# A memory-augmented transformer step on one core: an own buffer for the last head outputs of every fourth segment, and two steps of left-row work at other spots

## The chip, the cores and the metric

The kernel runs on one core of one Trainium2 chip. The metric is device time in microseconds (us), lower is better. Each time is one execution of the whole program; "before" is the median of three such runs. A profile is one further execution, with the hardware profiler on; it has its own, slightly longer time. Engines are named as in the profile: PE (TensorE, matmuls; PEld its weight loads), ACT (ScalarE), DVE (VectorE), POOL (GpSimd), SP (SyncE, which issues nearly all DMAs here; SPq in the profile).

## The reference, cut to what matters

```python
# x: 2048 tokens x 640; 32 heads of 192; segments of 32 tokens, 8 memory rows
for s in range(64):
    h = concatenate([mem, x[:, 32*s:32*s+32]])         # 40 rows
    q, k, v = h @ Wq, h @ Wk, h @ Wv                   # 40 x 32 heads x 192
    p = softmax(where(mask, q @ k.T / sqrt(192), -1e9))
    o = (p @ v) @ Wo                                   # 40 x 640
    mem = o[:, :8]                                     # the next segment needs this
    outs.append(o[:, 8:])
a = concatenate(outs)
b = (gelu(x @ w_gate) * (x @ w_up)) @ w_down
out = sigmoid((x * gate_w).sum(-1)) * a + (1 - that) * b
```

Segments form a chain: the first projection of a segment waits for the eight memory rows of the one before. The feed-forward part `b` is done ahead of the chain and isn't touched.

## The kernel before, in words

**Rows.** Of the 40 rows of a segment, the chain does 32 at once (24 tokens and the 8 memory rows). The last 8 tokens of a segment, its *left rows*, don't depend on the memory for their own queries, keys and values; they are done for four segments together, 32 rows again. Four segments make a group of places 0, 1, 2 and 3 (`q = s % 4`); there are 16 groups.

**Octets.** The 32 heads go through in four octets of eight heads, forwards in even segments, backwards in odd ones.

**Order.** Each segment walks a list written out by hand: `PROG` for places 0 and 2, `PROG1` (the same but for one item) for place 1, `PROG3` for place 3. Engines run their instructions in the order in which the list issues them; a layer records reads and writes of each region of on-chip memory and puts in the semaphore waits. Where a PE step waits for several engines, that layer may move all but one of the waits onto the last matmuls of the step in front. The items are

- `g n k`: step k (of 5) of projection group n, for queries, keys and values of some octets: four matmuls each (L1134, and L226 where the weights in the array are kept). When step 4 is done, ACT copies the result out (L1155 queries and keys, L1158 values)
- `tq`, `tk`: 32 x 32 transposes of queries and keys on DVE (L1172)
- `sc`, `ex`, `pt`: scores (PE, L1183 to L1198), softmax (DVE, ACT), transposes of the probabilities (PE, L1245 and L1250; ACT L1257 and L1263)
- `pv o`: probabilities times values of octet o (PE, L1278 and L1280, 12 matmuls on tiles of 128 x 64), and the copies of the head outputs to on-chip memory (ACT L1310 or, in two halves, L1300; DVE L1315 or, in two halves, L1304)
- `wo o h`: half of the output projection of octet o. At places 0 to 2 it takes 32 rows (PE, L1328; L1354 for the fourth octet, tiles of 128 x 32). At place 3 it is `wo_both` (PE, L1372, tiles of 128 x 64, 12 matmuls a half): 32 rows and the 32 left rows of the group, 64 columns of weights
- `lf x u k`: at place x alone, one of five steps of the queries and keys of left rows of the next group (a *left pair*: four matmuls at L926 and four at L226, tiles of 128 x 32); `le` copies the result out (ACT L1400, DVE L1402)
- `vb k`: at place 3, one of five steps of the left rows' values for the next segment (PE, L967, four matmuls on tiles of 128 x 32), copied out by ACT at L958

**Head outputs.** At places 0 to 2 two buffers `uT` alternate between octets, and the fourth octet is copied in two halves (two pairs of heads each), by ACT and DVE in parallel, so that the output projection can begin after the first. At place 3 there is one buffer, `U3` (1536 bytes a partition, 64 columns per head pair and part), over both `uT` buffers; POOL copies the left rows' head outputs of the group from `uTl` into its columns 40 to 64 (L1292), and ACT and DVE copy the octet in one piece each. As every octet uses the same buffer, the PV copies of octet o wait for the output projection of octet o - 1, and the list has `wo o-1 1` ahead of `pv o`.

**End of a segment.** After the last output projection the result is copied out (at place 3 ACT L1564 and DVE L1561), transposed on DVE (L1572) and becomes the memory rows of the next segment's first projection (L1134 again).

**Weights.** They don't all fit. In each segment 13 pieces of Wq, Wk and Wv and 3 of Wo are loaded over pieces that were used early in it, by SP (L631); each load waits for the last use of the slot and is used near the end of the segment. The three of Wo follow `wo 0 0` (two) and `wo 0 1` (one).

Of the kernel before, what the change touches and what calls it, by code (L numbers as in the profile page):

```python
# [238 lines left out]
def _build(nc, A_x, A_mem0, A_Wq, A_Wk, A_Wv, A_Wo, seg_len, w_gate, w_up, w_down,  # L239
# [124 lines left out]
    def sreg(o, nbytes, plo=0, phi=128):  # L364
        return Rg("sb", o, o + nbytes, plo, phi)
# [63 lines left out]
    r_U3p = [[sreg(wsB_off["uT"] + x + 4 * i, 4) for x in (0, UB)] for i in range(3)]  # L429
    st_f = [[fview(wsA_off["stats"] + (2 * b + i) * 16, 16) for i in (0, 0, 1)] for b in range(2)]  # L430
# [87 lines left out]
    def piece_view(key, o):  # L518
        if key[0] == 3:
# [76 lines left out]
    o = 0  # L596
# [669 lines left out]
    def pv_oct(s, o):  # L1266
# [23 lines left out]
        if q == 3:  # L1290
            u, ru = U3, r_U3p
            S_.add("pool", lambda e: e.tensor_copy(  # L1292
                out=U3.rearrange("p t c r -> p (t c) r")[:, :, R:64], in_=uTl[:, 12 * oc:12 * oc + 12, :]),
                reads=[r_uTl[oc]], writes=r_U3p[2], name="U3l s%d o%d" % (s, o))
        if o == NOCT - 2 and s + 1 < NSEG:
            ek_copy(s, (3,))
        if o == NOCT - 1 and q < 3:
            assert na == 2 and o % NUB == 1 and WOP == 4
            for h in ((0, 1), (1, 0))[s % 2]:
                S_.add("act", lambda e, h=h: e.activation(  # L1300
                    out=apx(u[:, 2 * h, 0, :], [[R, 2], [3 * R, 2], [1, R]]),
                    in_=ps[:, A, 0:2 * W].rearrange("p (c t r) -> p c t r", t=4, r=R)[:, :, 2 * h:2 * h + 2], func=ACTF.Copy),
                    reads=[r_ps[A]], writes=[r_uThp[h][0]], name="uT evac s%d o%d" % (s, o))
                S_.add("dve", lambda e, h=h: e.tensor_copy(  # L1304
                    out=u[:, 2 * h:2 * h + 2, 2, 0:R],
                    in_=ps[:, B, 2 * W:3 * W].rearrange("p (t r) -> p t r", r=R)[:, 2 * h:2 * h + 2]),
                    reads=[r_ps[B]], writes=[r_uThp[h][1]], name="uT mid s%d o%d" % (s, o))
# [60 lines left out]
    def wo_both(s, item):  # L1368
        for p in wo_pairs(s, item):
            g_, rg_ = piece(s, (3, p))  # L1370
            for c in range(3):
                S_.add("pe", [lambda e, i=i, g_=g_, c=c, p=p: e.matmul(  # L1372
                    ps[64 * i:64 * i + 64, LB, 0:2 * DJ], U3[:, p % 4, c, :], g_[:, c, 2 * DJ * i:2 * DJ * (i + 1)],
                    start=(p == NWP - 1 and c == 0), stop=(p == 0 and c == 2), tile_position=(0, 64 * i),
                    skip_group_check=True) for i in range(2)],
                    reads=[rg_, r_U3], writes=[r_ps[LB]], name="Wb s%d p%d" % (s, p))
# [4 lines left out]
    for x, prog in enumerate(PROGS):  # L1381
# [4 lines left out]
        assert all(at(("wo", i, 1)) < at(("pv", i + (1 if x == 3 else 2))) for i in range(NOCT - (1 if x == 3 else 2)))  # L1386
# [279 lines left out]
```

## Time and profile before

| what | before |
|---|---|
| three timed runs, median (lowest to highest) | 1659.49 us (1658.9 to 1665.99) |
| profiled execution: its time | 1669.24 us |
| profiled execution: span from first to last instruction | 1667.5 us |
| mean granted PE clock | 0.996 |
| the 64 segments in the span | from about 257.5 us to the end |
| the output matmuls of place 3 (L1372) | 1536, mean 307 ns, 122.6 us busy |
| POOL's copy of left rows at place 3 (L1292) | 64 of 128 x 288, 429 ns |
| loads of weight pieces, issue to landing (median) | 5.5 us Wq, 6.5 us Wk, 8.7 us Wv, 6.0 us Wo |

How to read it: the page gives busy time, share of the span and count per engine; the chain of waits follows the work that ended last back from the end. Timelines have rows of start (us from the start of the span), length (us), engine, line of the kernel, operation, tiles and count, and, in brackets, how long the engine had been idle before and what released it. Matmuls of one kind that follow each other are one row; matmuls are pipelined, so starts are better to calculate with than ends. Segment 25 (place 1), 26 (place 2) and 27 (place 3) start at 758.34, 780.83 and 803.58 us, segment 28 at 826.74.

### The profile page before, as it was taken

How to read it: one execution, taken by the hardware profiler on the slowest of the kernel's cores; microseconds unless marked ns; L12 is line 12 of the kernel's file. 1: busy time of each engine (PE TensorE's matmuls, PEld its weight loads, DVE VectorE, ACT ScalarE, POOL GpSimd, SP SyncE). 2: the span in 40 equal slices, each digit the busy share in tenths (PEclk: the TensorE clock that was granted, in tenths of full speed). 3: DMA queues.
4: the chain of work that ended last, by engine and by line, in shares of the span. 5: the costliest groups of instructions: out<-in, count | busy, mean ns of one | idle time of the engine just before them, and what ended most of it. 6: DMA issues, size and time to landing. Idle time of an engine off the chain costs nothing.

```text
span 1667.5 us, 75813 instructions
## 1 busy us (share of the span) xinstructions
PE 1566.5 (94%) x37107; PEld 779.2 (47%) x28147; DVE 1000.1 (60%) x3023; ACT 785.5 (47%) x1874; POOL 549.9 (33%) x1609
## 2 busy tenths in 40 slices
PE   9999899999999999999999999999999999999986
PEld 4444345444444445444455444454444454444533
DVE  6453566656566666666565666566665656656653
ACT  2222454545555454545455554455454555545442
POOL 1110233333333333333333333333333333333332
PEclk9999999999999999999999999999999999999999
DMA  9915899888889898988889898889888898888984
GB/s 297 340 43 160 323 321 330 301 282 310 324 317 325 300 319 290 334 306 311 303 305 343 315 327 289 303 315 340 308 302 310 308 336 311 307 297 308 324 312 179
DMA packets 275415, 499.28 MB, mean 299 GB/s; under 512 B 121119, under 2 KB 136327, under 8 KB 275079
## 3 DMA queue, kind: packets, MB, share of 16 engines
q1 hardware_dynamic: 271000, 491.30, 84.2%
q8 instruction: 255, 4.18, 1.0%
q10 hardware_dynamic: 4079, 3.14, 0.6%
q14 instruction: 81, 0.66, 0.1%
HBM read 473.25 MB, written 21.09 MB: 296 GB/s over the span
## 4 chain that ended last, share of the span: by engine, by line
PE 71%; DMA 17%; DVE 6%; ACT 3%; issue 3%; SPq 1%; POOL 0%; DVEq 0%; ACTq 0%; POOLq 0%
PE ps L1134 19%; PE ps L226 17%; DMA arena<-in_A_Wv_dram 9%; PE ps L1372 7%; DMA arena<-in_A_Wo_dram 6%; PE ps L1328 5%; PE ps L1278 3%; PE ps L835 3%; PE ps L832 3%; PE ps L1354 2%; PE ps L1183 2%; PE ps L926 2%; PE ps L858 2%; PE ps L1191 1%; DMA arena<-in_A_Wk_dram 1%
## 5 line engine op out<-in xcount | busy, mean ns | idle before, releaser
L1134 PE MATMUL ps<-arena 128*32 128x384 bf16 x8640 | 645.6, 328 | 28.0 <-DVE arena L1572 11.6
L226 PE MATMUL ps<-arena 128*32 128x384 bf16 x8960 | 639.7, 326 | 2.7 <-ACT arena L1155 1.2
L1134 PEld LDWEIGHTS ps<-arena 128*32 128x32 bf16 x8640 | 231.9, 96 | 399.2 <-issue 258.9
L1172 DVE STREAM_TRANSPOSE arena<-arena 128x384 bf16<-128x384 bf16 x512 | 273.6, 559 | 70.5 <-ACT arena L1155 69.3
L1155 ACT ACTIVATE arena<-ps 128x384 bf16<-128x384 f32 x512 | 230.4, 493 | 99.0 <-PE ps L1134 93.8
L1328 PE MATMUL ps<-arena 128*32 128x320 bf16 x3456 | 184.4, 300 | 16.2 <-issue 11.1
L1175 POOL COPY arena<-arena 64x160 bf16<-64x160 bf16 x256 | 81.9, 320 | 334.3 <-DVE arena L1172 332.8
L1210 DVE TENSOR_REDUCE arena<-ps 104x4 f32<-104x160 f32 x256 | 82.9, 324 | 162.3 <-PE ps L1198 162.0
L1158 ACT ACTIVATE arena<-ps 128x384 bf16<-128x384 f32 x256 | 124.9, 488 | 88.2 <-PE ps L1134 88.2
L1263 ACT ACTIVATE arena<-ps 128x448 bf16<-128x448 f32 x192 | 104.4, 544 | 125.3 <-PE ps L1250 125.3
L1222 ACT ACTIVATE ps<-ps 104x160 f32<-104x160 f32 x256 | 74.8, 292 | 177.0 <-DVE ps L1212 175.2
L1310 ACT ACTIVATE arena<-ps 128x480 bf16<-128x480 f32 (+1 forms) x208 | 116.7, 561 | 87.4 <-PE ps L1280 86.1
L1008 POOL COPY arena<-arena 128x96 bf16<-128x96 bf16 x256 | 70.2, 274 | 246.7 <-PE ps L1198 174.4
L1224 DVE TENSOR_REDUCE arena<-ps 104x4 f32<-104x160 f32 x256 | 82.9, 324 | 83.8 <-ACT ps L1222 82.4
L1372 PE MATMUL ps<-arena 128*64 128x320 bf16 x1536 | 122.6, 307 | 0.5 <-ACT arena L1310 0.5
L1278 PE MATMUL ps<-arena 128*64 128x160 bf16 x1536 | 116.9, 240 | 5.6 <-ACT arena L1155 3.4
L1328 PEld LDWEIGHTS ps<-arena 128*32 128x32 bf16 x3456 | 89.6, 96 | 62.2 <-issue 19.1
L926 PE MATMUL ps<-arena 128*32 128x384 bf16 x1280 | 109.6, 328 | 1.1 <-issue 0.8
L1280 PE MATMUL ps<-arena 128*64 128x64 bf16 x1536 | 103.7, 193 | 2.3 <-issue 1.9
L1400 ACT ACTIVATE arena<-ps 128x384 bf16<-128x384 f32 x120 | 57.3, 490 | 101.2 <-PE ps L926 48.9
L1318 POOL COPY arena<-arena 128x96 bf16<-128x96 bf16 x192 | 51.7, 270 | 159.8 <-ACT arena L1300 88.7
L1278 PEld LDWEIGHTS ps<-arena 128*64 128x64 bf16 x1536 | 81.2, 109 | 37.6 <-ACT arena L1158 14.4
(102 smaller groups left out, 2362.6 us busy)
## 6 DMA issues: line engine op xcount, KB each, us to landing
arena<-in_A_Wk_dram SPq DMA_DIRECT2D x335, 384.0 KB, 6.5
arena<-in_A_Wv_dram SPq DMA_DIRECT2D x335, 384.0 KB, 8.7
arena<-in_A_Wo_dram SPq DMA_DIRECT2D x205, 480.0 KB, 6.0
arena<-in_A_Wq_dram SPq DMA_DIRECT2D x209, 384.0 KB, 5.5
arena<-left_qk_scratch SPq DMA_DIRECT2D x126, 96.0 KB
left_qk_scratch<-arena SPq DMA_DIRECT2D x49, 192.0 KB, 5.4
left_qk_scratch<-arena SPq DMA_DIRECT2D x30, 96.0 KB, 5.5
ffn_b_scratch<-arena ACTq DMA_DIRECT2D x16, 160.0 KB, 4.1
```

The lines of the kernel that those rows point to most:

```text
L226: return e.add_instruction(mybir.InstMatmult(name=nm, start_tensor_calc=like["start"], stop_tensor_calc=stop, tile_size=(128, 32), tile_po ...
L926: fns.append(lambda e, outp=outp, rhs=rhs, j=j: e.matmul(outp, lhs, rhs, start=(k == 0), stop=(k == KT - 1), tile_position=(0, 32 * j)))
L1134: fns.append(lambda e, outp=outp, rhs=rhs, j=j: e.matmul(outp, lhs, rhs, start=(k == 0), stop=(k == KT - 1), tile_position=(0, 32 * j)))
L1155: S_.add("act", lambda e, m=m, bk=bk: e.activation(out=rows_sb[m], in_=ps[:, bk, 0:384], func=ACTF.Copy), reads=[r_ps[bk]], writes=[r_rows ...
L1158: S_.add("act", lambda e, i=i, bk=bk: e.activation(out=v_sb[i % NVB].rearrange("p (c n) -> p c n", c=3), in_=ps[:, bk, 0:384].rearrange("p ...
L1172: S_.add("dve", lambda e: e.transpose(out=dst[:, :, 0:L], in_=rows_sb[m].rearrange("p (c r) -> p c r", r=L)), reads=[r_rows[m]], writes=[r ...
L1263: S_.add("act", lambda e: e.activation(out=PT, in_=ps[:, bank, 0:PTW + 128], func=ACTF.Copy), reads=[r_ps[bank]], writes=[r_PT], name="pT ...
L1278: return [lambda e: e.matmul(full, v[:, e0:e0 + 64], PTm[:, i], start=True, stop=False, tile_position=(0, 64 * i), skip_group_check=True), ...
L1280: lambda e: e.matmul(part, vl[:, e0:e0 + 64], PTl[:, i], start=False, stop=True, tile_position=(0, 64 * i), skip_group_check=True)]
L1310: S_.add("act", lambda e: e.activation(out=apx(u[:, 0, 0, :], [[rs, na], [3 * rs, 4], [1, R]]), in_=ps[:, A, 0:na * W].rearrange("p (c t r ...
L1328: fns.append(lambda e, i=i, t=t, j=j, gv=gv: e.matmul(ps[32 * j:32 * j + 32, bank, 0:2 * DJ].rearrange("p (h n) -> p h n", h=2), lhs2[i], ...
L1372: S_.add("pe", [lambda e, i=i, g_=g_, c=c, p=p: e.matmul(ps[64 * i:64 * i + 64, LB, 0:2 * DJ], U3[:, p % 4, c, :], g_[:, c, 2 * DJ * i:2 * ...
```

## The change

Three things change.

1. At place 3 the fourth octet's head outputs get a buffer of their own, `U3h`: two halves of 768 bytes, one over the queries' buffer `Q`, one over the probabilities' buffer `p` (and what lies behind it, up to the keys), both out of use by then. POOL's copy of the left rows, ACT's copy and DVE's copy are done in halves, as at places 0 to 2; `wo_both` reads the half that holds its pair. That is one instruction more on each of POOL, ACT and DVE per segment of place 3.
2. In `PROG3`, `pv 3` moves ahead of `wo 2 1`, and the five `vb` all come behind `wo 3 1`. Before, `pv 3` came behind `wo 2 1`, three `vb` in front of `wo 3 0` and two behind `wo 3 1`.
3. In `PROG` (and so `PROG1`), the left pair `lf 2 1 2` of place 2 moves from behind `pv 3` to behind `sc 2`; the left pair `lf 1 1 2` of place 1 moves from in front of `pt 2` to behind `pv 3`. At place 1 that pair reads one weight piece from its copies in `ek` instead of its slot, since the slot's next load has been issued by then.

On PE the instructions are the same ones in another order; DMAs are the same, in the same order.

```diff
+    U3h = [bview(wsB_off[nm], 768).rearrange("p (t c r) -> p t c r", c=3, r=64) for nm in ("Q", "p")]
+    r_U3h = [sreg(wsB_off[nm], 768) for nm in ("Q", "p")]
+    r_U3hp = [[[sreg(wsB_off[nm] + x + 4 * i, 4) for x in xs_] for i in range(3)] for nm, xs_ in (("Q", (0, 8)), ("p", (0, 256, 512)))]
...
     PROG = [...
-            ("tk", 2), ..., ("sc", 2), ("ex", 2), ("pv", 1), ("wo", 0, 0),
+            ("tk", 2), ..., ("sc", 2), ("lf", 2, 1, 2), ("ex", 2), ("pv", 1), ("wo", 0, 0),
...
-            ("g", 5, 0), ("g", 5, 1), ("lf", 1, 1, 2), ("pt", 2), ("wo", 0, 1), ("tk", 3), ("sc", 3), ("pv", 2),
+            ("g", 5, 0), ("g", 5, 1), ("pt", 2), ("wo", 0, 1), ("tk", 3), ("sc", 3), ("pv", 2),
...
-            ("pt", 3), ("wo", 2, 1), ("pv", 3), ("lf", 2, 1, 2), ("lf", 0, 1, 1), ("lf", 0, 1, 2), ("wo", 3, 0),
+            ("pt", 3), ("wo", 2, 1), ("pv", 3), ("lf", 1, 1, 2), ("lf", 0, 1, 1), ("lf", 0, 1, 2), ("wo", 3, 0),
...
     PROG3 = [...
-            ("g", 5, 4), ("wo", 2, 0), ("wo", 2, 1), ("pv", 3), ("vb", 0), ("vb", 1), ("vb", 2), ("wo", 3, 0),
-            ("wo", 3, 1), ("vb", 3), ("vb", 4)]
+            ("g", 5, 4), ("wo", 2, 0), ("pv", 3), ("wo", 2, 1), ("wo", 3, 0), ("wo", 3, 1), ("vb", 0), ("vb", 1),
+            ("vb", 2), ("vb", 3), ("vb", 4)]
...
-        if q == 3:
+        if q == 3 and o < NOCT - 1:
             u, ru = U3, r_U3p
             S_.add("pool", lambda e: e.tensor_copy(
                 out=U3.rearrange("p t c r -> p (t c) r")[:, :, R:64], in_=uTl[:, 12 * oc:12 * oc + 12, :]),
                 reads=[r_uTl[oc]], writes=r_U3p[2], name="U3l s%d o%d" % (s, o))
+        if q == 3 and o == NOCT - 1:
+            for h in ((0, 1), (1, 0))[s % 2]:
+                S_.add("pool", lambda e, h=h: e.tensor_copy(
+                    out=U3h[h].rearrange("p t c r -> p (t c) r")[:, :, R:64], in_=uTl[:, 12 * oc + 6 * h:12 * oc + 6 * h + 6, :]),
+                    reads=[r_uTl[oc]], writes=r_U3hp[h][2], name="U3l s%d o%d" % (s, o))
...
-        if o == NOCT - 1 and q < 3:
+        if o == NOCT - 1:
+            uh, rh, rs = ([u[:, 2 * h:2 * h + 2] for h in range(2)], [[[x] for x in y] for y in r_uThp], R) if q < 3 else (U3h, r_U3hp, 64)
             for h in ((0, 1), (1, 0))[s % 2]:
                 S_.add("act", lambda e, h=h: e.activation(
-                    out=apx(u[:, 2 * h, 0, :], [[R, 2], [3 * R, 2], [1, R]]),
+                    out=apx(uh[h][:, 0, 0, :], [[rs, 2], [3 * rs, 2], [1, R]]),
...
                 S_.add("dve", lambda e, h=h: e.tensor_copy(
-                    out=u[:, 2 * h:2 * h + 2, 2, 0:R],
+                    out=uh[h][:, :, 2, 0:R],
...
     def wo_both(s, item):
         for p in wo_pairs(s, item):
             g_, rg_ = piece(s, (3, p))
+            u, ru = (U3h[p % 4 // 2][:, p % 2], r_U3h[p % 4 // 2]) if item[1] == NOCT - 1 else (U3[:, p % 4], r_U3)
...
-                    reads=[rg_, r_U3], writes=[r_ps[LB]], name="Wb s%d p%d" % (s, p))
+                    reads=[rg_, ru], writes=[r_ps[LB]], name="Wb s%d p%d" % (s, p))
```

More of the change, by code (lines that the diff above doesn't have):

```diff
@@ L1385, in _build @@
         assert at(("sc", 2)) < at(("pv", 1))
-        assert all(at(("wo", i, 1)) < at(("pv", i + (1 if x == 3 else 2))) for i in range(NOCT - (1 if x == 3 else 2)))
+        assert all(at(("wo", i, 1)) < at(("pv", i + (1 if x == 3 else 2))) for i in range(NOCT - 2))
         n_wos.append(at([item for item in prog if item[0] not in ("lf", "le", "vb")][-1]))
```

9 lines of the change are left out of this document (5 added, 4 removed), and 16 rows, old and new, of the table PROG.

## The prediction

> **What bounds the kernel now.** First the page: its time, who is busy, and the chain that ended last.
>
> ```profile
> span 1667.5 us, 75813 instructions
> PE 1566.5 (94%) x37107; PEld 779.2 (47%) x28147; DVE 1000.1 (60%) x3023; ACT 785.5 (47%) x1874; POOL 549.9 (33%) x1609
> ...
> PE 71%; DMA 17%; DVE 6%; ACT 3%; issue 3%; SPq 1%; POOL 0%; DVEq 0%; ACTq 0%; POOLq 0%
> ```
>
> The profiled execution took 1669.24 us around this span; the three timed runs have a median of 1659.49 (1658.9 to 1665.99), 0.6% less. I add up against 1669.24 and carry the ratio over. PE is busy 94% and carries 71% of the chain: time can come only from PE's idle gaps. DMA is second, so the view of stretches comes next, for the 64 segments alone (us, busy times, granted clock, DMA share, GB/s):
>
> ```profile
> 257.50:1667.50 1410.00, 1321.57 (x34040) 663.75 (x25712) 862.03 (x2713) 700.24 (x1699) 504.87 (x1482) 1.00 0.87 308
> ```
>
> The granted clock is 1.00, so no gap is a throttled clock, and the DMA engines are 87% busy: a gap that closes can reopen as a wait for a weight piece. The view of waits tells which gaps there are (us in total, times, longest):
>
> ```profile
> PE ps L1134 <- DVE arena L1572: 11.6, 18, 0.7
> ...
> PE ps L1134 <- DMA arena<-in_A_Wv_dram: 8.8, 23, 0.7
> ...
> PE ps L1354 <- DMA arena<-in_A_Wo_dram: 6.9, 15, 0.9
> ```
>
> The first is the next segment's projection waiting for the memory transposes; 23 and 15 are V pieces and Wo pieces that land after PE is ready. No single gap is large: the change must be worked out place by place, on the timeline.
>
> **Place 3.** This is the end of segment 27 (start, length, engine, line).
>
> ```profile
> 820.67 0.34 PE L1134 MATMUL ps<-arena 128*32 128x384 bf16 x4
> ...
> 820.93 1.82 PE L1372 MATMUL ps<-arena 128*64 128x320 bf16 x24
> ...
> 821.08 0.29 POOL L807 COPY arena<-arena 128x120 bf16<-128x120 bf16 x1 [0.17 <-PE ps L1134]
> 821.19 0.48 ACT L1158 ACTIVATE arena<-ps 128x384 bf16<-128x384 f32 x1
> ...
> 822.59 0.23 PE L1278 MATMUL ps<-arena 128*64 128x160 bf16 x2
> ...
> 822.76 0.20 PE L1280 MATMUL ps<-arena 128*64 128x64 bf16 x2
> ...
> 822.78 0.24 PE L1278 MATMUL ps<-arena 128*64 128x160 bf16 x2
> ...
> 822.86 0.20 PE L1280 MATMUL ps<-arena 128*64 128x64 bf16 x2
> ...
> 822.98 0.94 PE L967 MATMUL ps<-arena 128*32 128x384 bf16 x12
> 823.09 0.44 ACT L1310 ACTIVATE arena<-ps 128x320 bf16<-128x320 f32 x1 [1.42 <-PE ps L1280]
> ...
> 823.58 0.10 PEld L967 LDWEIGHTS ps<-arena 128*32 128x32 bf16 x2 [0.33 <-ACT arena L1310]
> 823.85 1.82 PE L1372 MATMUL ps<-arena 128*64 128x320 bf16 x24
> ...
> 825.61 0.51 PE L967 MATMUL ps<-arena 128*32 128x384 bf16 x8
> ...
> 826.43 0.58 DVE L1572 STREAM_TRANSPOSE arena<-arena 128x64 bf16<-128x64 bf16 x2
> ...
> 826.74 0.35 PE L1134 MATMUL ps<-arena 128*32 128x384 bf16 x4 [0.62 <-DVE arena L1572]
> ```
>
> Read downwards: last V step, 24 output matmuls (wo 2,0 and wo 2,1), the fourth octet's PV, three vb steps, a wait of 0.33 for the head outputs on ACT, the last 24 output matmuls, two vb steps, a wait of 0.62 for the transposes, the next segment.
>
> The 24 output matmuls take 822.59 - 820.93 = 1.66 us, 0.069 each, twelve 0.83. PV to the next matmul is 0.39. In the new order:
>
> - PV can start after twelve, at 821.76. It needs the V copy on ACT, which ends at 821.19 + 0.48 = 821.67: 0.09 to spare. **No wait**, but narrowly (first rival).
> - PV is now followed by output matmuls of its own tile shape. Between its pairs PE goes on within 0.02 us (822.76 to 822.78); leaving for the vb shape took 0.12 (822.86 to 822.98). I take 0.10 as the price of a change of shape, the same as V to output matmuls (820.67 to 820.93 is 0.26, where four matmuls of that kind take 0.16, see place 1). So PV lasts 0.29, to 822.05. The Trainium skill, "TensorEngine Tiling (Array Packing)", Key Properties, says that changing the tiling mode drains TensorE; without it the gain below would be 0.87 a segment, 1.6 us less in all, and at place 2 it counts against the change. The trace agrees, with the 0.10.
> - Twelve output matmuls (wo 2,1) fill 822.05 to 822.88. Meanwhile ACT and DVE evacuate in halves. In places 0 to 2 the same two halves begin 0.57 us after PV's start and take 0.50 together (rows under place 1), so the first is done about 0.82 after PV, an estimate: 822.58, ahead of 822.88. The second, 822.83, is wanted twelve matmuls later. ACT, DVE and POOL issue one instruction more each; POOL's two copies have no wait behind the x copy, which ends at 821.37, and 1.5 us until they are wanted. The second ACT half also waits for the second POOL copy (four shared bytes in the dependency regions); that copy comes straight behind the first, so it costs nothing. **The wait of 0.33 goes.**
> - The last 24 run from 822.88 to 824.54; before, 823.85 to 825.51. **Saved: 0.97 us.**
> - From the last output matmul to the next segment: 826.74 - 825.51 = 1.23, a chain through ACT, DVE and the transposes that doesn't get shorter. All five vb steps now lie under it: 0.10 + 5 x 0.16 = 0.92. The wait that is left is 0.31 instead of 0.62; the vb steps have moved from in front of the chain to beside it. What is late next is this chain.
>
> Sixteen segments (the last has no vb, but the same wait to lose): 16 x 0.97 = **15.5 us**, bounds 0 and 16 x 0.97.
>
> The last piece of Wo is a DMA, and now wanted 0.97 earlier. First and last of the fifteen such loads (segments 3 and 59): issue and landing, then its first use.
>
> ```profile
> L631 SPq DMA_DIRECT2D arena<-in_A_Wo_dram x1: 328/328/328, 260.8 to 260.8; - x1
> ...
> DMA to landing us min/median/max: 8.0/8.0/8.0
> ...
> 269.32 0.57 PE L1372 MATMUL ps<-arena 128*64 128x320 bf16 x6
> ...
> L631 SPq DMA_DIRECT2D arena<-in_A_Wo_dram x1: 328/328/328, 1552.1 to 1552.1; - x1
> ...
> DMA to landing us min/median/max: 7.8/7.8/7.8
> ...
> 1560.55 0.57 PE L1372 MATMUL ps<-arena 128*64 128x320 bf16 x6
> ```
>
> Landed 0.5 and 0.65 us ahead (268.8 for 269.32, 1559.9 for 1560.55). Over the fifteen the margin goes from 0.54 to 2.69 us; five are under 0.97 (0.54, 0.63, 0.65, 0.73, 0.90) and wait for the rest: 0.43 + 0.34 + 0.32 + 0.24 + 0.07 = **1.4 us given back**. The load's issue depends on wo 0,1, which isn't moved.
>
> **Place 1.** The pair leaves the spot before pt 2 and goes behind the fourth PV (segment 25).
>
> ```profile
> 772.50 0.82 PE L1134 MATMUL ps<-arena 128*32 128x384 bf16 x16
> ...
> 773.15 0.34 PE L926 MATMUL ps<-arena 128*32 128x384 bf16 x4
> ...
> 773.86 0.54 DVE L1172 STREAM_TRANSPOSE arena<-arena 128x384 bf16<-128x384 bf16 x1
> ...
> 774.45 0.15 PEld L1191 LDWEIGHTS ps<-arena 128*40 128x40 bf16 x6 [0.27 <-DVE arena L1172]
> ...
> 778.24 0.26 PE L1278 MATMUL ps<-arena 128*64 128x160 bf16 x2
> ...
> 778.81 0.50 ACT L1300 ACTIVATE arena<-ps 128x160 bf16<-128x160 f32 x2
> ...
> 779.17 1.01 PE L1354 MATMUL ps<-arena 128*32 128x160 bf16 x48 [0.44 <-DVE arena L1304]
> ```
>
> Four of these matmuls take (773.15 - 772.50)/4 = 0.16, a pair 0.33. Taking it out brings sc 3 nothing: the scores start at 774.45, when the key transpose ends (773.86 + 0.54 = 774.40), and that hangs on DVE, not on the pair. The wait in front of sc 3 grows by 0.33. Behind PV the pair then lies in the wait of 0.44, and the output matmuls start when the copy is there, 0.93 after PV as now (place 2, which has the pair there, shows 0.98). **0 us**; bounds: 16 x 0.05 lost, and a gain up to the part of the 6.9 us of Wo waits that falls here, since wo 0,1 frees the last Wo slot 0.33 earlier. Behind the moved pair nothing but PE's own output matmuls is queued.
>
> **Place 2.** The pair goes behind sc 2, between two steps of the other shape: 0.33 + 2 x 0.10 = 0.53 us on PE.
>
> ```profile
> 794.61 0.50 PE L1134 MATMUL ps<-arena 128*32 128x384 bf16 x5 [0.25 <-DMA arena<-in_A_Wv_dram]
> ...
> 795.58 0.35 PE L1134 MATMUL ps<-arena 128*32 128x384 bf16 x4 [0.48 <-DMA arena<-in_A_Wv_dram]
> ...
> 800.08 0.26 PE L1278 MATMUL ps<-arena 128*64 128x160 bf16 x2
> ...
> 801.06 0.53 PE L1354 MATMUL ps<-arena 128*32 128x160 bf16 x15
> ...
> 887.28 1.03 DVE L1172 STREAM_TRANSPOSE arena<-arena 128x384 bf16<-128x384 bf16 x2
> ```
>
> In segment 26 PE then waits 0.25 + 0.48 = 0.73 us for V pieces: the pair lies in it. With 23 such waits, two a segment, some eleven of sixteen segments are like this. In the others (segment 30) sc 3 hangs on the transposes that end at 888.31; the keys behind the pair are 0.53 later, but DVE has about 0.2 of slack there, so sc 3 comes about 0.3 later: 5 x 0.3 = 1.5. Most of it falls into later waits of the same segment (last Wo piece, 15 waits of 6.9/15 = 0.46). I take **0.5 us lost**; bounds 0 and 16 x 0.53 = 8.5. Taking the pair from behind PV costs nothing: output matmuls start 0.98 after PV with it, 0.93 without it (place 1). The first two Wo loads are issued 0.53 later at most, behind a queue of V loads that PE itself is waiting for.
>
> **Sum:** 15.5 - 1.4 - 0.5 = 13.6; 1669.24 - 13.6 = 1655.6; on the median 1659.49 x 1655.6/1669.24 = **1646.0 us**.
>
> **Rivals.**
>
> 1. *PV at place 3 waits for the V copy.* For: 0.09 us to spare, and PE took 823.85 - 823.53 = 0.32 from the end of an ACT copy to the matmuls behind it. Against: there, vb matmuls stood between. Price 0.32 - 0.09 = 0.23: 16 x 0.74 = 11.8, less 0.7 of DMA and 0.5: gain 10.6, 1649.0 us.
> 2. *Place 2 pays in full*: its V waits follow the later work instead of swallowing it. Gain 13.6 + 0.5 - 8.5 = 5.6, 1653.9 us. Against: the waits end with a landing.
> 3. *The change doesn't do what it says*: the DMA queue returns place 3's gain as waits for pieces in places 0 and 1. For: 87% busy. Against: margins of 0.5 us and more at the end of place 3. 1659.5 us.
> 4. *Slower*: the same return, and at place 2 landings follow issues, so the 0.53 by which wo 0,0 and its loads come later moves the last Wo piece, and with it the segment's end: 16 x 0.53 = 8.5, 1659.5 + 8.5 = 1668 us. It decides from the point where the queue is empty when these loads are issued. Against: 8 us from issue to landing is a queue, and a load that stands in a queue can be issued later at no cost.
>
> **How the numbers follow.** Forecast 0.62, rival 1 0.15, rival 2 0.12, rival 3 0.05, rival 4 0.06. A measurement of this kernel can tell about 0.5%, 8.3 us: below 1651.2 is faster, above 1667.8 slower. Faster 0.62 + 0.15 = 0.77; within 0.12 + 0.05 = 0.17; slower 0.06. Range: the low end has no loss at places 2 and 3 and 3 us of place 1's Wo waits (13.6 + 1.9 + 3 = 18.5): 1641; the high end takes in rival 2: 1654.5. Left out are rivals 3 and 4, 0.11, and the tails.
>
> **What would show it.** Right: at the end of place 3, PV twelve output matmuls earlier, no wait between the output matmuls, five vb steps under the chain and about 0.3 left before the next segment, so the 11.6 us of L1134 on L1572 fall to about 7; new small waits of L1372 for Wo, 1.4 us; the 0.44 behind PV shows at place 2 instead of place 1; place 1's wait before sc 3 grows by 0.33; the V waits of 8.8 shrink. Wrong: a gap before PV at place 3 (rival 1), place 2 longer by half a microsecond (2), V or Wo waits that grow at places 0 and 1 (3, 4).

## The result, and the profile after

| | before | after |
|---|---|---|
| median of 11 runs each, on the same chip | 1663.14 us | 1651.77 us |
| ratio, 95% interval | | 0.9933 (0.9913 to 0.9954) |
| profiled execution: its time | 1669.24 us | 1657.64 us |
| profiled execution: span, granted clock | 1667.5 us, 0.996 | 1655.8 us, 0.995 |

The change makes the kernel faster by 0.67%, 11.1 us of 1663.14. A second set of twelve runs of the changed kernel gave 0.9944 (0.9923 to 0.9964). One of the eleven runs of the changed kernel took 2936.64 us and isn't in the ratio.

The forecast was 1646.0 us, range 1641 to 1654.5, a ratio of 1655.6/1669.24 = 0.9918 to the kernel before. 1651.77 us lies in the range, and 0.9918 in the interval. Of the 5.8 us between the two times, 3.6 come from the kernel before, whose median is 1663.14 us in eleven runs and was 1659.49 in the first three; the rest is gain that was forecast and didn't come.

The page of the profile after: the span, the busy times, and the chain that ended last by engine.

```profile
span 1655.8 us, 75860 instructions
...
PE 1562.1 (94%) x37107; PEld 776.2 (47%) x28147; DVE 999.1 (60%) x3039; ACT 784.7 (47%) x1890; POOL 552.6 (33%) x1625
...
PE 69%; DMA 15%; DVE 8%; ACT 4%; issue 3%; SPq 1%; POOL 0%; DVEq 0%; ACTq 0%; POOLq 0%
```

PE has the same 37107 instructions; what went is idle time. Lines have moved: the projection L1134 is now L1138, the output matmuls of place 3 L1372 are L1383, those of the fourth octet at places 0 to 2 L1354 are L1364, the memory transposes L1572 are L1583, the vb steps L967 are L971, PV L1278 and L1280 are L1282 and L1284. The view of waits after (us in total, times, longest):

```profile
PE ps L1364 <- DMA arena<-in_A_Wo_dram: 6.8, 14, 0.9
...
PE ps L1138 <- DMA arena<-in_A_Wv_dram: 3.0, 7, 0.8
...
PE ps L1138 <- DVE arena L1583: 2.2, 7, 0.7
...
PE ps L1383 <- DMA arena<-in_A_Wo_dram: 0.9, 2, 0.6
```

Against before: the wait for the memory transposes fell from 11.6 to 2.2, that for V pieces from 8.8 to 3.0; the wait for the last Wo piece at places 0 to 2 stayed (6.9 to 6.8); one for Wo at place 3 is new. It is larger than this view says, as is shown below. The end of segment 27 on the timeline after:

```profile
813.29 0.34 PE L1138 MATMUL ps<-arena 128*32 128x384 bf16 x4
...
813.55 1.01 PE L1383 MATMUL ps<-arena 128*64 128x320 bf16 x12
...
813.81 0.48 ACT L1162 ACTIVATE arena<-ps 128x384 bf16<-128x384 f32 x1
...
814.39 0.24 PE L1282 MATMUL ps<-arena 128*64 128x160 bf16 x2
...
814.69 2.63 PE L1383 MATMUL ps<-arena 128*64 128x320 bf16 x36
...
814.90 0.50 ACT L1310 ACTIVATE arena<-ps 128x160 bf16<-128x160 f32 x2 [0.60 <-PE ps L1284]
814.90 0.39 DVE L1314 CAST arena<-ps 128x80 bf16<-128x80 f32 x2 [1.07 <-PE ps L1284]
...
817.25 1.00 PE L971 MATMUL ps<-arena 128*32 128x384 bf16 x20
...
818.08 0.58 DVE L1583 STREAM_TRANSPOSE arena<-arena 128x64 bf16<-128x64 bf16 x2
...
818.38 0.28 PEld L1138 LDWEIGHTS ps<-arena 128*32 128x32 bf16 x8 [0.52 <-DVE arena L1583]
```

Read downwards: twelve output matmuls, PV at 814.39, then 36 output matmuls in one row without a wait between them, the five vb steps, the next segment. PV lasts 814.69 - 814.39 = 0.30 us to the next output matmul. Both halves of the head outputs are out by 814.90 + 0.50 = 815.40; the first is wanted at 814.69 + 12 x 0.068 = 815.51, when the last 24 output matmuls begin.

**One measure for all runs.** The work of place 3 from the start of wo 2 0 (its last 48 output matmuls) to the next segment falls into two parts. Part A goes from the start of wo 2 0 to the start of the last 24 output matmuls, part B from there to the next segment's first projection. Before: A = 823.85 - 820.93 = 2.92, B = 826.74 - 823.85 = 2.89. After: A = 815.51 - 813.55 = 1.96, B = 818.38 - 815.51 = 2.87. In segment 27 A fell by 0.96 (forecast 0.97) and B, the last 24 matmuls and the chain behind them, did not move.

Segment 27 stands for all of them in A (1.96 in every segment of place 3 in the profile after), but not in B. Over the fifteen groups that have a next segment, B is 2.89 in the mean before and 3.03 after. The chain behind the last matmul is the same, 1.36 to 1.41 us from its start to the next projection in every one of these segments. What grew is the stretch of the 24 matmuls, at the first pair of the last Wo piece. PEld, the weight loads, shows it: first a row of the timeline after, in segment 15, then the line of its view of waits (before has no such line).

```profile
542.39 0.28 PEld L1383 LDWEIGHTS ps<-arena 128*64 128x64 bf16 x6 [0.38 <-DMA arena<-in_A_Wo_dram]
...
PEld ps L1383 <- DMA arena<-in_A_Wo_dram: 3.5, 9, 1.0
```

PE's own view lists two of these nine waits, since it counts idle time from the modelled end of the matmul before and leaves out what is short. By the starts of the matmuls, the last piece holds them up by 2.1 us in all after and 2.0 in the second set; before, by nothing.

The length of a segment is measured between the ends of the second memory transposes (DVE L1572, or its line in the kernel in question) of successive segments, in the one profiled execution; the table has the mean over segments 4 to 62 of each place (14 or 15 segments).

| kernel | ratio to before (95%) | place 0 | 1 | 2 | 3 | part A, segment 27 |
|---|---|---|---|---|---|---|
| before | | 23.34 | 23.03 | 22.46 | 23.37 | 2.92 |
| after | 0.9933 (0.9913 to 0.9954) | 23.60 | 22.98 | 22.52 | 22.52 | 1.96 |
| after, second set | 0.9944 (0.9923 to 0.9964) | 23.51 | 22.90 | 22.08 | 22.60 | |
| place 3 alone | 0.9926 (0.9901 to 0.9951) | 23.39 | 22.76 | 22.04 | 22.68 | |
| pairs alone | 1.0009 (0.9987 to 1.0030) | 23.29 | 22.83 | 22.55 | 23.18 | |
| buffer alone | 0.9993 (0.9974 to 1.0012) | 23.30 | 22.76 | 22.37 | 23.10 | 2.79 |
| old buffer, vb behind | 1.0016 (1.0001 to 1.0031) | 23.31 | 22.81 | 22.31 | 23.46 | 3.18 |
| buffer, PV early | 0.9995 (0.9972 to 1.0019) | 23.47 | 22.94 | 22.21 | 22.94 | 2.66 |
| buffer, vb behind | 0.9969 (0.9952 to 0.9986) | 23.38 | 22.86 | 22.16 | 22.78 | 2.55 |
| after without both pairs | 0.9898 (0.9873 to 0.9923) | 23.21 | 22.84 | 22.17 | 22.49 | |
| after, place 2's pair back | 0.9930 (0.9903 to 0.9957) | 23.20 | 22.82 | 22.27 | 22.42 | |
| after without vb | 0.9993 (0.9975 to 1.0011) | 24.15 | 22.67 | 22.53 | 22.41 | |
| after with two of five vb | 0.9927 (0.9905 to 0.9949) | 23.52 | 22.72 | 22.41 | 22.48 | |

The two rows of the changed kernel show how far a place's mean goes from one execution to the next: 0.44 us at place 2, about 0.1 at the others. Place 3 moves by more than that; place 0 moves clearly in one run alone, the one without vb.

### The profile page after: what moved, and what is told of

Read it like the earlier page. It is cut to its first block, busy times and chain, and to the rows that moved or that the text cites. A ratio compares the mean times of both kernels' runs of the same rounds, so it can differ in the third digit from the quotient of the medians.

```text
span 1655.8 us, 75860 instructions
## 1 busy us (share of the span) xinstructions
PE 1562.1 (94%) x37107; PEld 776.2 (47%) x28147; DVE 999.1 (60%) x3039; ACT 784.7 (47%) x1890; POOL 552.6 (33%) x1625
## 4 chain that ended last, share of the span: by engine, by line
PE 69%; DMA 15%; DVE 8%; ACT 4%; issue 3%; SPq 1%; POOL 0%; DVEq 0%; ACTq 0%; POOLq 0%
PE ps L1138 19%; PE ps L226 17%; DMA arena<-in_A_Wo_dram 8%; PE ps L1383 6%; PE ps L1338 5%; DMA arena<-in_A_Wk_dram 3%; PE ps L1282 3%; PE ps L839 3%; PE ps L836 3%; DMA arena<-in_A_Wv_dram 3%; PE ps L930 2%; PE ps L1187 2%; PE ps L1364 2%; PE ps L862 2%; DVE arena L1176 2%
## 5 line engine op out<-in xcount | busy, mean ns | idle before, releaser
L1138 PE MATMUL ps<-arena 128*32 128x384 bf16 x8640 | 640.1, 328 | 14.2 <-DMA arena<-in_A_Wv_dram 3.0
L226 PE MATMUL ps<-arena 128*32 128x384 bf16 x8960 | 641.0, 326 | 3.3 <-ACT arena L1159 1.2
L1138 PEld LDWEIGHTS ps<-arena 128*32 128x32 bf16 x8640 | 228.6, 96 | 382.8 <-issue 265.1
L1320 ACT ACTIVATE arena<-ps 128x480 bf16<-128x480 f32 x192 | 109.7, 571 | 60.7 <-PE ps L1284 60.7
L1282 PE MATMUL ps<-arena 128*64 128x160 bf16 x1536 | 118.3, 240 | 5.7 <-ACT arena L1159 3.4
L1383 PE MATMUL ps<-arena 128*64 128x320 bf16 x1536 | 122.2, 304 | 1.0 <-DMA arena<-in_A_Wo_dram 0.9
L1284 PE MATMUL ps<-arena 128*64 128x64 bf16 x1536 | 104.0, 193 | 3.4 <-issue 3.4
L1282 PEld LDWEIGHTS ps<-arena 128*64 128x64 bf16 x1536 | 81.3, 109 | 44.9 <-ACT arena L1162 19.5
```

The lines of the kernel that those rows point to most:

```text
L226: return e.add_instruction(mybir.InstMatmult(name=nm, start_tensor_calc=like["start"], stop_tensor_calc=stop, tile_size=(128, 32), tile_po ...
L1138: fns.append(lambda e, outp=outp, rhs=rhs, j=j: e.matmul(outp, lhs, rhs, start=(k == 0), stop=(k == KT - 1), tile_position=(0, 32 * j)))
L1282: return [lambda e: e.matmul(full, v[:, e0:e0 + 64], PTm[:, i], start=True, stop=False, tile_position=(0, 64 * i), skip_group_check=True), ...
L1284: lambda e: e.matmul(part, vl[:, e0:e0 + 64], PTl[:, i], start=False, stop=True, tile_position=(0, 64 * i), skip_group_check=True)]
L1320: S_.add("act", lambda e: e.activation(out=apx(u[:, 0, 0, :], [[rs, na], [3 * rs, 4], [1, R]]), in_=ps[:, A, 0:na * W].rearrange("p (c t r ...
L1383: S_.add("pe", [lambda e, i=i, g_=g_, c=c, p=p, u=u: e.matmul(ps[64 * i:64 * i + 64, LB, 0:2 * DJ], u[:, c, :], g_[:, c, 2 * DJ * i:2 * DJ ...
```

## The experiments

The theory to be tested was the prediction's: the gain is made at place 3, by PV and wo 2 1 in another order and by vb steps put under the chain, and the two pairs carry none of it. The rivals: the pairs make or cost something (rival 2), or only one part of the place 3 change matters.

**Place 3 alone.** `PROG` as before; buffer and `PROG3` as after.

```diff
     PROG = [...
-            ("sc", 2), ("lf", 2, 1, 2), ("ex", 2), ...
+            ("sc", 2), ("ex", 2), ...
-            ("g", 5, 1), ("pt", 2), ...
+            ("g", 5, 1), ("lf", 1, 1, 2), ("pt", 2), ...
-            ("pv", 3), ("lf", 1, 1, 2), ("lf", 0, 1, 1), ...
+            ("pv", 3), ("lf", 2, 1, 2), ("lf", 0, 1, 1), ...
```

> Place 3 as changed, both left pairs back where they were. Theory (all of the gain is place 3's, the pairs move work into waits): 15.5 - 1.4 = 14.1 us less than before, ratio 0.9915, and place 3's median segment 0.9 us shorter as in the changed kernel (22.3 against 23.2 us). Rival (the pairs carry a part of the gain): ratio 0.996 or more. Rival (the pairs cost their full 0.53 us at place 2): this version beats the changed one by 8 us, ratio 0.988.

Measured: 0.9926 (0.9901 to 0.9951). Place 3 alone has all that the whole change has, as far as the intervals tell.

**Pairs alone.** The kernel before with the `PROG` of after.

```diff
-            ("sc", 2), ("ex", 2), ("pv", 1), ...
+            ("sc", 2), ("lf", 2, 1, 2), ("ex", 2), ("pv", 1), ...
-            ("g", 5, 1), ("lf", 1, 1, 2), ("pt", 2), ...
+            ("g", 5, 1), ("pt", 2), ...
-            ("pv", 3), ("lf", 2, 1, 2), ("lf", 0, 1, 1), ...
+            ("pv", 3), ("lf", 1, 1, 2), ("lf", 0, 1, 1), ...
```

> Only the two left pairs moved, place 3 as before. Theory: no difference that can be measured, ratio 1.000 (0 to 0.5 us more); place 1 and 2 keep their median segments (22.9 and 22.6 us) within 0.1 us, place 3 stays at 23.2 us. Rival (place 2 pays in full): 8.5 us more, ratio 1.005, place 2 at 23.1 us. Rival (the pairs gain): ratio 0.997 or less.

Measured: 1.0009 (0.9987 to 1.0030), so the 0.5% of rival 2 is out. The view of waits of this kernel (lines as before) shows where the moved pair of place 2 lies:

```profile
PE ps L1134 <- DMA arena<-in_A_Wv_dram: 2.9, 6, 1.0
```

The waits for V pieces are 2.9 us in 6 places where the kernel before has 8.8 in 23: PE now comes later to the pieces, and by this view 5.9 of the pair's 16 x 0.53 = 8.5 us is time that PE waited anyway. The run without both pairs, below, finds less covered.

**Buffer alone.** Own buffer and halves, both lists as before.

```diff
-            ("g", 5, 4), ("wo", 2, 0), ("pv", 3), ("wo", 2, 1), ("wo", 3, 0), ("wo", 3, 1), ("vb", 0), ("vb", 1),
-            ("vb", 2), ("vb", 3), ("vb", 4)]
+            ("g", 5, 4), ("wo", 2, 0), ("wo", 2, 1), ("pv", 3), ("vb", 0), ("vb", 1), ("vb", 2), ("wo", 3, 0),
+            ("wo", 3, 1), ("vb", 3), ("vb", 4)]
```

> The own buffer and the copies in halves at place 3 alone, with the old order (three vb steps behind the fourth PV, two at the end; the fourth PV behind both halves of the output projection before it). Theory: the first half is copied about 0.8 us after PV's start, the three vb steps end 0.9 us after it, so the wait of 0.33 in front of the last output matmuls goes and nothing else: place 3 gets 0.3 us shorter (22.9 us), 16 x 0.3 = 5 us, ratio 0.997. Rival (the buffer makes the whole gain): ratio 0.992. Rival (the buffer does nothing without the order): ratio 1.000.

Measured: 0.9993 (0.9974 to 1.0012); part A is shorter by 0.13 us, less than half of what was expected. The timeline of segment 27:

```profile
812.65 1.82 PE L1383 MATMUL ps<-arena 128*64 128x320 bf16 x24
...
814.31 0.24 PE L1282 MATMUL ps<-arena 128*64 128x160 bf16 x2
...
814.70 0.81 PE L971 MATMUL ps<-arena 128*32 128x384 bf16 x12
814.82 0.50 ACT L1310 ACTIVATE arena<-ps 128x160 bf16<-128x160 f32 x2 [1.42 <-PE ps L1284]
...
815.17 0.10 PEld L971 LDWEIGHTS ps<-arena 128*32 128x32 bf16 x2 [0.19 <-ACT arena L1310]
815.44 1.50 PEld L1383 LDWEIGHTS ps<-arena 128*64 128x64 bf16 x24 [0.17 <-DVE arena L1314]
815.44 1.82 PE L1383 MATMUL ps<-arena 128*64 128x320 bf16 x24
...
818.33 0.35 PE L1138 MATMUL ps<-arena 128*32 128x384 bf16 x4 [0.62 <-DVE arena L1583]
```

The wait for the copies isn't in front of the output matmuls, it is inside the vb steps: two of their weight loads, at 815.17, carry the wait for ACT's half (the layer that moves waits onto the step in front). So the rest of that vb step and the change of shape still come behind ACT's copy, and then a load waits 0.17 for DVE's half. And the wait before the next segment is 0.62, as before.

**Old buffer, vb behind.** The other half of the change alone: the vb steps go behind, the buffer stays shared, so PV must stay behind wo 2 1.

```diff
-            ("g", 5, 4), ("wo", 2, 0), ("wo", 2, 1), ("pv", 3), ("vb", 0), ("vb", 1), ("vb", 2), ("wo", 3, 0),
-            ("wo", 3, 1), ("vb", 3), ("vb", 4)]
+            ("g", 5, 4), ("wo", 2, 0), ("wo", 2, 1), ("pv", 3), ("wo", 3, 0), ("wo", 3, 1), ("vb", 0), ("vb", 1),
+            ("vb", 2), ("vb", 3), ("vb", 4)]
```

> All five vb steps behind the last output matmuls, with the old buffer, the copies in one piece and the fourth PV behind both halves of the output projection before it. Theory: the wait behind PV is uncovered (PV to the output matmuls about 1.0 us instead of 1.26, no vb in it), the wait for the transposes falls from 0.62 to 0.3 us: place 3 gets 0.25 us shorter, 4 us, ratio 0.9975. Rival (moving the vb steps is the whole gain): ratio 0.993. Rival (it only uncovers a wait): 1.000 or more.

Measured: 1.0016 (1.0001 to 1.0031), the other sign. The timeline of segment 27 (lines as before):

```profile
813.94 1.82 PE L1372 MATMUL ps<-arena 128*64 128x320 bf16 x24
...
815.59 0.24 PE L1278 MATMUL ps<-arena 128*64 128x160 bf16 x2
...
815.86 0.19 PE L1280 MATMUL ps<-arena 128*64 128x64 bf16 x1
815.90 0.43 POOL L1292 COPY arena<-arena 128x288 bf16<-128x288 bf16 x1 [1.52 <-PE ps L1372]
...
816.38 0.22 PE L1280 MATMUL ps<-arena 128*64 128x64 bf16 x1 [0.33 <-POOL arena L1292]
...
816.63 0.44 ACT L1310 ACTIVATE arena<-ps 128x320 bf16<-128x320 f32 x1 [1.95 <-PE ps L1280]
...
817.12 1.82 PE L1372 MATMUL ps<-arena 128*64 128x320 bf16 x24 [0.53 <-ACT arena L1310]
...
820.01 0.35 PE L1134 MATMUL ps<-arena 128*32 128x384 bf16 x4
```

The last matmul of PV waits for POOL's copy of the left rows, which had to wait for the last reader of the shared buffer, wo 2 1. The view says 0.33; by starts it comes 816.38 - 815.86 = 0.52 after the matmul before it, its twin on the other tile, where the other twins come 0.003 after each other. PV ends late, ACT's copy starts at 816.63, 1.04 after PV's start (before: 823.09 - 822.59 = 0.50), and the output matmuls come 1.53 after it instead of 1.26. The view of waits shows that it is so in every segment of place 3:

```profile
PE ps L1280 <- POOL arena L1292: 4.6, 16, 0.3
```

Before, this wait is there once (0.3 us): three vb steps stood behind PV, and the wait for POOL lay on them. This theory was formed from the trace; the next experiment but one tests it.

**Buffer, PV early.** As place 3 alone, but with three vb steps in front of the last output matmuls.

```diff
-            ("g", 5, 4), ("wo", 2, 0), ("pv", 3), ("wo", 2, 1), ("wo", 3, 0), ("wo", 3, 1), ("vb", 0), ("vb", 1),
-            ("vb", 2), ("vb", 3), ("vb", 4)]
+            ("g", 5, 4), ("wo", 2, 0), ("pv", 3), ("wo", 2, 1), ("vb", 0), ("vb", 1), ("vb", 2), ("wo", 3, 0),
+            ("wo", 3, 1), ("vb", 3), ("vb", 4)]
```

> Own buffer with its halves, and PV of the fourth octet ahead of wo 2 1 at place 3; three vb steps in front of the last output matmuls as before; left pairs as before. Theory: only the wait for the head outputs goes (0.24 us of it were left with the buffer alone) and the vb steps stay in front of the chain, so that the wait of 0.6 to 0.8 before the next segment stays: 0.3 us a segment less than before, place 3 at about 22.9, 16 x 0.3 = 4.8 us, ratio 0.997. Rival (moving PV is what brings the gain, and the vb steps' spot does not matter): the whole 0.92 us, place 3 at 22.3, ratio 0.991 to 0.993.

Measured: 0.9995 (0.9972 to 1.0019) for an expected 0.997, just outside the interval; place 3 at 22.94 for 22.9. The timeline:

```profile
813.25 1.01 PE L1383 MATMUL ps<-arena 128*64 128x320 bf16 x12
...
815.31 0.67 PE L971 MATMUL ps<-arena 128*32 128x384 bf16 x12
815.91 1.50 PEld L1383 LDWEIGHTS ps<-arena 128*64 128x64 bf16 x24 [0.32 <-issue]
815.91 1.82 PE L1383 MATMUL ps<-arena 128*64 128x320 bf16 x24
...
818.80 0.35 PE L1138 MATMUL ps<-arena 128*32 128x384 bf16 x4 [0.63 <-DVE arena L1583]
```

No wait for the copies is left, and A is 815.91 - 813.25 = 2.66, 0.26 less than before (16 x 0.26 = 4.2 us, a ratio of 0.9975, which the interval allows), but the vb steps stand in front (815.31 to 815.91), and 0.63 of waiting is left behind them. The rival, that moving PV brings the whole gain, falls.

**Buffer, vb behind.** As old buffer, vb behind, with the own buffer; the list is that one's.

> Own buffer with its halves, all five vb steps behind the last output matmuls at place 3, but PV of the fourth octet behind wo 2 1 as before; left pairs as before. It differs from the run with the old buffer and all vb behind (place 3 longer by 0.26 us, ratio 1.0016) in the buffer alone. Theory (that loss came from PV's last matmul waiting for POOL's copy of the left rows, which had to wait for wo 2 1 in the shared buffer): with an own buffer PV is not held, the last output matmuls start about 0.95 us after PV's start, as the fourth octet's at places 0 to 2 do, instead of 1.27 in the kernel before and 1.53 in that run; place 3 at about 22.9, 16 x 0.32 = 5.1 us, ratio 0.997. Rival (the loss came from the bare copies in front of the output matmuls, whatever the buffer): place 3 as before or longer, ratio 1.000 to 1.002.

Measured: 0.9969 (0.9952 to 0.9986), as expected. The timeline:

```profile
815.15 1.82 PE L1383 MATMUL ps<-arena 128*64 128x320 bf16 x24
...
816.80 0.24 PE L1282 MATMUL ps<-arena 128*64 128x160 bf16 x2
...
817.31 0.50 ACT L1310 ACTIVATE arena<-ps 128x160 bf16<-128x160 f32 x2 [1.42 <-PE ps L1284]
817.67 1.53 PEld L1383 LDWEIGHTS ps<-arena 128*64 128x64 bf16 x24 [0.55 <-ACT arena L1310]
817.70 1.82 PE L1383 MATMUL ps<-arena 128*64 128x320 bf16 x24 [0.43 <-DVE arena L1314]
...
820.58 0.35 PE L1138 MATMUL ps<-arena 128*32 128x384 bf16 x4
```

ACT's copy starts 0.51 after PV's start instead of 1.04, the output matmuls 0.90 instead of 1.53. With the same list, the own buffer with its halves makes 3.18 into 2.55. Of these 0.63, 0.53 is ACT's copy, which no longer stands behind POOL's: that was the loss of the old buffer. The other 0.10 may be the copies in halves; no run has the own buffer without them. What is left is a wait of 0.43 behind PV, with nothing to fill it.

So part A is 2.92 before, 2.66 with PV early, 2.55 with vb behind, and 1.96 with both. From the 2.79 of the buffer alone, the one brings 0.13, the other 0.24, both together 0.83. The 2.66 - 1.96 = 0.70 between PV early and both is what the three vb steps and two changes of shape take, 3 x 0.16 + 2 x 0.10 = 0.68. The vb steps were the cover for the copies; they can only leave when something else covers them, and that is wo 2 1 behind PV, which the shared buffer doesn't allow.

**Without vb, and with two of five vb.** The changed kernel with the vb steps left out: first all five (the left rows' values of place 0's first octet are then missing in fifteen groups), then three.

```diff
-            ("g", 5, 4), ("wo", 2, 0), ("pv", 3), ("wo", 2, 1), ("wo", 3, 0), ("wo", 3, 1), ("vb", 0), ("vb", 1),
-            ("vb", 2), ("vb", 3), ("vb", 4)]
+            ("g", 5, 4), ("wo", 2, 0), ("pv", 3), ("wo", 2, 1), ("wo", 3, 0), ("wo", 3, 1)]
```

> The changed kernel with the five vb steps left out (left rows' values of seven segments in eight are then wrong or stale). Theory (the five steps lie beside the chain of copies and transposes from the last output matmul to the next segment, and cost nothing there): place 3 stays at 22.3 within 0.1 us, the wait before the next segment grows from 0.33 by the 0.9 us of the steps, and the ratio to the changed kernel is 1.000, that is 0.993 to before; only the V pieces used by the steps could be reloaded earlier, which may take a little from waits at place 0. Rival (the steps still hold up the end of place 3 in part): up to 16 x 0.9 = 14 us less, ratio about 0.985.

Measured: 0.9993 (0.9975 to 1.0011): slower than the kernel that does the work. Place 3 is 22.41, as expected, but place 0 went from 23.60 to 24.15. The view of waits (lines one less than after):

```profile
PE ps L226 <- ACT arena L1158: 23.9, 48, 0.9
PE ps L1137 <- DVE arena L1582: 18.2, 18, 1.1
```

The second row is the expected one: the wait before the next segment takes up the time of the steps. The first was 1.2 us in 3 places in the changed kernel. The vb steps take a PSUM bank from a rotation, and without them PE meets banks that ACT hasn't copied out yet. The second version keeps the rotation:

```diff
-                    vl_mm(s + 1, i)
+                    if i in (0, 4):
+                        vl_mm(s + 1, i)
```

> The changed kernel with three of the five vb steps left out (the middle ones; the left rows' values of one octet per group then miss three fifths of their sum), so that PSUM banks rotate as in the changed kernel; with all five left out, the rotation shifted and place 0 got new waits for banks. Theory (the steps lie beside the chain of copies and transposes): place 3 stays at 22.3 within 0.1 us, place 0 at 23.4 within 0.2, the wait before the next segment grows from 0.33 by 3 x 0.16 = 0.48 to about 0.8, ratio to the changed kernel 1.000, to before 0.993. Rival (the steps hold up the end in part): up to 16 x 0.48 = 7.7 us less, ratio to before 0.989.

Measured: 0.9927 (0.9905 to 0.9949), beside 0.9944 for the changed kernel in the same set; places 0 and 3 are 23.52 and 22.48, those of the changed kernel 23.60 and 22.52. The view of waits, and the start of segment 28:

```profile
PE ps L1138 <- DVE arena L1584: 11.3, 18, 0.7
```

```profile
815.50 0.51 PE L971 MATMUL ps<-arena 128*32 128x384 bf16 x8
...
816.62 0.35 PE L1138 MATMUL ps<-arena 128*32 128x384 bf16 x4 [0.62 <-DVE arena L1584]
```

The time of the three steps turned into waiting, 2.2 us to 11.3 in all, and the waits of L226 for ACT are back at 1.0 us in 2 places: the loss at place 0 came with the shifted rotation. The three steps cost nothing where they are in the changed kernel, within the 0.3% of this comparison.

**Without both pairs.** The changed kernel with both moved pairs left out; this takes 0.86 us of PE from places 1 and 2.

```diff
-            ("sc", 2), ("lf", 2, 1, 2), ("ex", 2), ...
+            ("sc", 2), ("ex", 2), ...
-            ("pv", 3), ("lf", 1, 1, 2), ("lf", 0, 1, 1), ...
+            ("pv", 3), ("lf", 0, 1, 1), ...
```

> The changed kernel with both moved left pairs left out altogether (the eight matmuls of one step of the left queries and keys at place 1 and at place 2; the left queries and keys of those octets are then wrong). PE has 0.33 us less to do at place 1 and 0.33 plus two changes of shape, 0.53, at place 2. Theory (both pairs lie in waits that end with something else: the key transpose and the V copy at place 1, V and Wo pieces at place 2): the medians of places 1 and 2 stay within 0.15 us of 22.98 and 22.51, and the ratio to before is that of the changed kernel, 0.993, at most 0.002 lower. Rival (PE sets these two places): 0.86 us x 16 = 13.8 us less, ratio about 0.985.

Measured: 0.9898 (0.9873 to 0.9923), 0.0035 and 0.0046 below the two sets of the changed kernel, that is 5.8 and 7.7 us. It lies between the theory (at most 3.3 us) and the rival (13.8): part of the pairs' PE time is covered and part is not, about half and half by these numbers. The intervals (each 3.5 to 4 us either way) don't allow more. In the table, 0.42 of the 0.91 us by which the four places together are shorter than in the first execution of the changed kernel lie at places 0 and 3, where nothing was left out, so the means by place don't settle it either.

**Place 2's pair back.** The changed kernel with that pair behind PV again, and beside it the changed kernel itself.

```diff
-            ("sc", 2), ("lf", 2, 1, 2), ("ex", 2), ...
+            ("sc", 2), ("ex", 2), ...
-            ("pv", 3), ("lf", 1, 1, 2), ("lf", 0, 1, 1), ...
+            ("pv", 3), ("lf", 2, 1, 2), ("lf", 1, 1, 2), ("lf", 0, 1, 1), ...
```

> The changed kernel with the left pair of place 2 back behind the fourth PV; the pair of place 1 stays in its new spot. Theory A (moving it costs some: in the new spot 0.53 us of PE time is covered only in part by the V pieces' waits, and the spot behind PV that it left was covered by the copies; place 2 was 22.45 us in the mean with the new spot and 22.24 in the mean of the runs with the old): place 2 shorter by about 0.2 us, 3.4 us in all, ratio to before 0.991 where the changed kernel has 0.993. Theory B, the prediction's (0.5 us in all): the same as the changed kernel within 0.001. Rival (rival 2 of the prediction, the place pays in full): 8.5 us less, ratio 0.988.

> The changed kernel itself, so that the runs of this call and the one without the two pairs have it beside them. Theory: ratio to before 0.993 again, place 2 about 22.4 to 22.5 us in the mean, place 1 about 22.9. If it lies at 0.990 or 0.996, differences of 0.003 between runs of other calls say nothing.

Measured: 0.9930 (0.9903 to 0.9957) and 0.9944 (0.9923 to 0.9964). The difference, 0.0014 or 2.3 us, is within the intervals: theories A (3.4 us) and B (0.5 us) aren't told apart, and the 8.5 us of rival 2 are unlikely. Place 2 of the changed kernel was 22.08 in this execution and 22.52 in the other, so the 0.2 us on which theory A stood is within scatter. No version that does all the work is shown to beat the changed kernel: place 3 alone and this one are level with it.

## Why the prediction was right, and where it was off

1. **PV ahead of wo 2 1 without a wait (rival 1).** Right. The V copy ends at 813.81 + 0.48 = 814.29, 0.10 before PV; forecast 0.09. PV starts at 814.39, 0.84 after the twelve matmuls began.
2. **PV to the next output matmul 0.29.** Right: 0.30, against 0.39 before. The Trainium skill, "TensorEngine Tiling (Array Packing)", Key Properties, says that a change of the tiling mode drains TensorE; the trace agrees in that a change between these two shapes costs about 0.10 us. The 36 matmuls and the change to vb fit it too: 817.25 - 814.69 = 2.56, and 36 x 0.068 + 0.10 = 2.55.
3. **The wait of 0.33 goes; 0.97 saved a segment.** Right: A fell by 0.96 in segment 27. Place 3 fell by 0.85 and 0.77 in the mean of the two executions; most of the difference is the Wo waits of point 5, which lie in B.
4. **The chain of 1.23 doesn't get shorter, 0.31 is left.** Right: from the start of the last output matmul to the next projection it takes 1.36 to 1.41 us in every group, before and after. The last vb step starts at about 817.25 + 4 x 0.16 = 817.9, would be done for the next matmul at 818.07, and the projection starts at 818.38. The sign that went with it was wrong: 11.6 did not fall to about 7 but to 2.2. The view counts idle time from the modelled end of the last matmul (0.35 long where the next can start after 0.16), so a wait of 0.31 shows as little or nothing. Starts carry the argument, not that view. (0.10 + 5 x 0.16 is 0.90; the forecast's 0.92 is this sum before rounding, and doesn't matter.)
5. **DMA gives back 1.4 at place 3.** Right in kind, too small here. PE's view lists 0.9 us in two waits (0.7 in two in the second set), but by starts it is 2.1 us and 2.0 us, in nine and eight groups of fifteen; the forecast had five, from the margins of one execution. The seven executions with this end of place 3 go from 0.9 to 2.7, so the margins of one were not enough to tell.
6. **Place 1: nothing.** Not refuted: 22.98 and 22.90 for 23.03. In the profile after, the key transpose of segment 25 ends at 765.08 and the scores follow it, with a wait for it, at 765.14. From the sixteen projection matmuls in front to the scores it is 765.14 - 763.19 = 1.95 us, and 774.45 - 772.50 = 1.95 before, with the pair in between:

```profile
763.19 0.82 PE L1138 MATMUL ps<-arena 128*32 128x384 bf16 x16
...
764.55 0.53 DVE L1176 STREAM_TRANSPOSE arena<-arena 128x384 bf16<-128x384 bf16 x1
...
765.14 0.28 PE L1195 MATMUL ps<-arena 128*40 128x40 bf16 x8 [0.22 <-DVE arena L1176]
```

7. **Place 2: 0.5 us lost.** The mechanism is there (V waits 8.8 to 3.0), the size isn't settled. Behind PV, output matmuls start 0.98 after PV as before, now with a wait of 0.49 in place of the pair, and the last Wo piece is still waited for:

```profile
791.84 0.26 PE L1282 MATMUL ps<-arena 128*64 128x160 bf16 x2
...
792.82 0.77 PE L1364 MATMUL ps<-arena 128*32 128x160 bf16 x23 [0.49 <-ACT arena L1310]
...
793.91 0.32 PE L1364 MATMUL ps<-arena 128*32 128x160 bf16 x8 [0.32 <-DMA arena<-in_A_Wo_dram]
```

8. **The sum.** Forecast 13.6 us of 1669.24; measured 11.1 and 9.3 us of 1663.14, and 12.3 for place 3 alone. The term that is known best is nearly right: place 3 brought 16 x 0.85 and 16 x 0.77, 13.6 and 12.3 us, against 15.5 - 1.4 = 14.1. The Wo waits of point 5 take 0.6 to 0.7 us more than forecast. Of the 2.5 and 4.3 us that the whole gain lacks, most isn't located. Term 7 may hold some of it: the pairs alone made the kernel 1.5 us longer, and putting place 2's pair back gained 2.3, for a forecast of 0.5, but neither is clear of its interval. Place 0 has means of 23.60 and 23.51 for 23.34; three kernels with the same end of place 3 have 23.20 to 23.39 there, so no cause is shown. That 1651.77 us lies in the range owes something to its width, which was made for place 2 paying in full: by the forecast's own line, faster below 1651.2, it is just not faster, and only the eleven runs of both kernels show that it is.

Rivals 3 (DMA takes the gain back) and 4 (slower) fell: at place 3 only 2.1 us came back, and the waits for Wo at places 0 to 2 stayed at 6.8 in PE's view.

## What to carry to other kernels

Steps that stand between a producer and its consumer may be there as cover. Before moving them to a better spot, ask which waits lie under them, all of them, and what else can stand in their place: here the vb steps covered ACT's copies and a POOL copy that the view of waits of the kernel before listed only once, and moving them alone made part A longer by 0.26 us. A cover and its replacement must be moved together, and here a buffer of its own made the replacement possible. To cost work by leaving it out, keep the rotation of banks and buffers as it was: leaving out all five steps shifted it and lost the whole gain. And where a gain is counted in short waits, compare the starts of instructions in every segment, and not the view of idle time or one segment alone.

## What the runs showed of the hardware that was not expected

- PE has idle stretches for which the profile shows no cause. The largest group, in the view of waits of before:

```profile
PE ps L1328 <- issue: 11.1, 17, 1.5
```

  From 175 us on, all PE waits of this kind in that view come to 22.6 us in 39 places before, and in the other profiles to between 13.1 (without vb) and 25.4 (after: 25.0 in 44). They are up to 1.7 us long and not at the same places in each group of four segments. They are of the size of the differences that could not be settled here.
- A view of PE's idle time shows short waits too small or not at all. In old buffer, vb behind, the last matmul of PV starts 0.52 us after its twin and ACT's copy comes 0.54 us later than before (1.04 for 0.50 after PV's start), while the view has a wait of 0.33. For the last Wo piece at place 3 after, PE's view has 0.9 us in two places, PEld's 3.5 in nine, and the starts of the matmuls say 2.1.
